# T5 attention and a feed-forward layer on one core: tail keys' scores as 64x64 products, and a bank hand-over that waits in TensorE's queue

## The chip, the cores and the metric

The kernel runs on one core of one Trainium2 chip. The metric is device time in microseconds of one execution, the median of several runs. TensorE (PE) multiplies matrices, VectorE (DVE) and ScalarE (ACT) work on rows of 128 partitions, GpSimd (POOL) and SyncE (SP) here mostly start transfers. PEld is TensorE's loading of weights, the operand that stays in the array; it overlaps with its products.

## The reference

Attention with a bias by distance for 8 batches, 8 heads, 576 positions and 64 numbers a head, then a feed-forward layer on the 4608 tokens:

```python
scores = scale * np.matmul(q, k.transpose(0, 1, 3, 2))
scores = scores + bias.transpose(2, 0, 1)[None, :, :, :]     # bias_table[bucket of |i - j|]
attn = np.exp(scores - np.max(scores, axis=-1, keepdims=True))
attn = attn / (np.sum(attn, axis=-1, keepdims=True) + 1e-09)
x = np.matmul(attn, v)            # heads side by side: 4608 x 512
h = x @ w_in                      # 512 x 2048
out = np.maximum(0.01 * h, h) @ w_out
```

## The kernel before

**Work items.** Two heads of one batch form a pair; 32 pairs n = 0 to 31 are worked through in order. Keys and queries of a pair lie transposed in SBUF, head e on partitions 64e to 64e + 63 (`kt`, `qt`). The 576 positions make four blocks of 128 (NJ = 4) and a tail of 64 (SL).

**Scores.** `score(n, u)` is `qk_mm` (TensorE) and then `exp` (ScalarE). For u = 0 to 3 it takes key block u against the first 512 queries, one product of 64 rows for each head, side by side in the array (64\*128 in the profile: rows by columns of the array). u = 4 takes all four blocks against the last 64 queries (eight small products, L314), u = 5 the 64 tail keys against all queries. For u = 5 the two heads' tail keys are put into one block-diagonal 128x128 operand by `apart` (VectorE, L284), which `transpose_k` calls; then two full-array products run, 512 and 64 columns wide (L324, L325). Scores 0, 1, 2, 3 and 5 rotate through two buffers `ps_s` of two PSUM banks each, so scores 5 wait for the exponential of scores 2.

**Values.** `av_tails` (L370) and `av_phase` (L416) multiply the exponentials with the values into one PSUM bank for each head; `divide` normalises.

**Feed-forward.** Its pieces (`ffn_in`, L468; `ffn_out`, L509) are laid between the steps of the pairs. Which kind and how many is fixed by a small planner (`plan`, `groups_of`, `two_kinds`).

**Halved pairs.** In 19 of the pairs (8, 9, 12 to 14, 17 to 19, 21 to 31) `two_kinds` chooses `body_in_halves`. There the value products, and two feed-forward pieces (`side_by_side`, L628), are split by rows of the array: the upper 64 rows work for one bank while the lower 64 work for the other, and in a second half they change over. Before the change-over the last product of the first half must have ended, because the other rows then write the same bank. `fence` puts a nop on SyncE that waits for that product, and `behind` makes the first product of the second half wait for the nop. In program order TensorE's stream of such a pair is: scores 0, value tails, first half of the values, scores 1, first products of the two feed-forward pieces, second half of the values, rest of the pieces' first half, scores 2, scores 3, the pieces' second half (four products a piece, as in the first), scores 4, one quarter of `ffn_out`, scores 5, more feed-forward work. All engines' orders are written out by hand (a manual schedule).

Functions that the change touches:

Of the kernel before, what the change touches and what calls it, by code (L numbers as in the profile page):

```python
# [37 lines left out]
def kernel(  # L38
# [10 lines left out]
    nc = tc.nc  # L49

    B, H, S, D = q.shape
# [4 lines left out]
    P = 128  # L56
    n_pairs = H // 2
    NJ = S // P
    SL = S - NJ * P
# [5 lines left out]
    n_cc = DM // P  # L65
# [178 lines left out]
    qts, kts, ops_ = {}, {}, {}  # L244
    N = len(items)
    AHEAD = 3

    prs, turned = {}, {}

# [8 lines left out]
    def by_dma(n):  # L258
        return n > 2 * n_pairs
# [22 lines left out]
    def apart(t):  # L282

        nc.vector.tensor_tensor(  # L284
            out=t[:, S : S + P].rearrange("p (e i) -> p e i", e=2),
            in0=t[:, NJ * P : S].unsqueeze(1).to_broadcast([P, 2, SL]),
            in1=own, op=ALU.mult)
# [6 lines left out]
    def transpose_k(n):  # L294
        kt = kts[n] = kts_[n % 2]
        t = turned_pair(n, 1)
        cuts = [0, -(-P // NC), RQ] if n == 0 else [0, RQ]
        for lo, hi in zip(cuts, cuts[1:]):
            nc.vector.tensor_copy(out=kt[:, lo * NC : hi * NC].rearrange("p (r c) -> p r c", c=NC),
                                  in_=t[:, lo:hi, :])  # L300
        apart(kt)

    def qk_mm(n, u, swapped=False):

        qt, kt = qts[n], kts[n]
        if u == NJ:
            if swapped:
                ps = [ps_m_pool.tile([P, 512], FP32, name="ps_q", tag="m") for e in range(2)]
            else:
                ps = [ps_o_pool.tile([P, 512], FP32, name="ps_q", tag=f"o{e}") for e in range(2)]  # L310
            for c in range(NJ):
                for e in range(2):
                    r = slice(e * D, (e + 1) * D)
                    nc.tensor.matmul(ps[e][:, c * SL : (c + 1) * SL], lhsT=kt[r, c * P : (c + 1) * P],  # L314
                                     rhs=qt[r, 512:S], start=True, stop=True)
            return ps
        ps = ps_s_pool.tile([P, 2, 512], FP32, name="ps_s")
        if u < NJ:
            for e in range(2):
                r = slice(e * D, (e + 1) * D)  # L320
                nc.tensor.matmul(ps[:, e, :], lhsT=kt[r, u * P : (u + 1) * P], rhs=qt[r, 0:512],  # L321
                                 start=True, stop=True)
        else:
            nc.tensor.matmul(ps[:, 0, :], lhsT=kt[:, S : S + P], rhs=qt[:, 0:512], start=True, stop=True)  # L324
            nc.tensor.matmul(ps[:, 1, 0:SL], lhsT=kt[:, S : S + P], rhs=qt[:, 512:S], start=True, stop=True)  # L325
        return ps

    def at_view(n):
        return at_[n % 2][:, 0:ATW].rearrange("p (e c i) -> p e c i", e=2, c=NJ)

    def exp(n, u, ps):
        at, at4 = at_view(n), at4_[n % 2]
        if u < NJ:
            nc.scalar.activation(at[:, :, u, 0:512], ps, AF.Exp, scale=scale)  # L334
        elif u == NJ:
            for e in range(2):
                nc.scalar.activation(at[:, e, :, 512:S],  # L337
                                     ps[e][:, 0 : NJ * SL].rearrange("p (c i) -> p c i", i=SL),
                                     AF.Exp, scale=scale)
        else:  # L340
            nc.scalar.activation(at4[:, 0:S], ps.rearrange("p e i -> p (e i)")[:, 0:S], AF.Exp, scale=scale)  # L341
# [54 lines left out]
    ended = mybir.DependencyInfo(mybir.DependencyClass.Sync, mybir.DependencyReason.DATA)  # L396

    def fence(sooner):

        f = nc.sync.nop(nofuse=True)  # L400
        tc.add_manual_dep(f.ins, sooner.ins.name, ended, reason="behind the last products of these rows")
        return f

    def behind(later, f):
        tc.add_manual_dep(later.ins, f.ins.name, ended, reason="the other half of the rows writes this bank")

    def av_phase(n, phase, last=None):

        b, p = items[n]
        at = at_[n % 2]  # L410
        for ic in range(NJ + 1):
            for c in range(NJ):
                for r in range(2):
                    e = r ^ phase
                    o = (e * NJ + c) * S + ic * P
                    m = nc.tensor.matmul(outs[n][e][:, ic * (D + 1) : (ic + 1) * (D + 1)],  # L416
                                     lhsT=at[halves[r], o : o + P], rhs=vn[b % NBUF][halves[r], c, 2 * p + e, :],
                                     start=False, stop=(phase == 1 and ic == NJ and c == NJ - 1))
                    if last is not None:
                        behind(m, last)  # L420
                        last = None
        return m

    def x_by_dma(n):
        return n_pairs + 2 <= n < N - 1 and n != 2 * n_pairs - 1
# [195 lines left out]
    def side_by_side(one, two):  # L621

        def phase(k, lo, hi, last=None):
            for c in range(lo, hi):
                for r in range(2):
                    pm, steps, low = one if r == k else two
                    w, x = steps[c]
                    m = nc.tensor.matmul(pm, lhsT=w[halves[r]], rhs=x[halves[r]], start=(k == 0 and c == 0),  # L628
                                         stop=(low is not None and k == 1 and c == n_cc - 1))
                    if last is not None:  # L630
                        behind(m, last)
                        last = None
            return m

        return phase
# [11 lines left out]
    def body_in_halves(n, kinds):  # L647

        late_loads = items[n][1] == 1
        if not late_loads:  # L650
            loads(n)
        turns = rows_ahead(n) if by_dma(n + 1) else []
        score(n, 0)
        av_tails(n - 1)
        last = fence(av_phase(n - 1, 0))
        score(n, 1)
        T, s = made["out"], at_piece["out"]
        if kinds[0] == "out":
            one, two = open_piece("out", (T, s)), open_piece("out", (T, s + 4))
        else:  # L660
            one, two = open_piece("in"), open_piece("out")
        phase = side_by_side(one, two)
        phase(0, 0, 1)
        av_phase(n - 1, 1, last)
        late_q = n == 2 * n_pairs
        if n + 1 < N and not late_q:
            transpose_q(n + 1)
        band(n, 0)
        divide(n - 1, range(2))
        if late_q:  # L670
            transpose_q(n + 1)
        if late_loads:
            loads(n, 1)
        last = fence(phase(0, 1, n_cc))
        score(n, 2)
        score(n, 3)
        phase(1, 0, n_cc, last)
        band(n, 1)
        if n + 1 < N:
            transpose_k(n + 1)  # L680
        score(n, 4)
        if kinds[0] == "in":
            one[2]()
        late = [n - 1]
        if x_by_dma(n - 1):
            x_transposes(late.pop())
        for m in turns:
            turn_by_dma(m)
        while stores:
            o, y = stores.pop(0)  # L690
            nc.sync.dma_start(out=o, in_=y)
        band(n, 2)
        if kinds[0] == "out":
            outs_pm[T] = one[0]
            ffn_out(T, s + 1)
            band(n, 4)
            score(n, 5)
            band(n, 5)
            ffn_out(T, s + 2)
            ffn_out(T, s + 3)  # L700
            for m in late:
                x_transposes(m, "o0")
                finished(m)
            outs_pm[T] = two[0]
            for part in range(5, 8):
                ffn_out(T, s + part)
            at_piece["out"] = (s + 8) % n_fc
            made["out"] += at_piece["out"] == 0
            return
        piece_out()  # L710
        band(n, 4)
        score(n, 5)
        band(n, 5)
        piece_out()
        piece_out()
        for m in late:
            x_transposes(m, "o1")
            finished(m)
        room["left"] -= 5
        moe(room["left"], 0)  # L720
# [91 lines left out]
    def rows_ahead(n):  # L812
        ms = [m for m in range(n + 2, min(n + AHEAD + 1, N))
              if by_dma(m) and m - (AHEAD if m > 2 * n_pairs + 2 else 2) == n]
        for m in ms:
            pair_rows(m)
        return ms
# [5 lines left out]
    def score(n, u):  # L823
        exp(n, u, qk_mm(n, u))
# [78 lines left out]
    n = n_pairs  # L903
# [25 lines left out]
    for n in range(n_pairs + 1, N + 1):  # L929
# [43 lines left out]
        while stores:  # L973
            o, y = stores.pop(0)
# [8 lines left out]
        if room["only"]:  # L983
# [6 lines left out]
            T, f = step("in")  # L990
# [54 lines left out]
```

## Time and profile before

| | |
|---|---|
| median of 3 runs | 370.56 us (370.3, 370.56, 372.05) |
| span of the profiled execution | 368.2 us |
| the profiled execution's own time | not given beside its span |
| busy: TensorE, ScalarE, VectorE, GpSimd | 97%, 67%, 53%, 20% of the span |
| granted TensorE clock | 1.000 |

The span runs from the first to the last instruction. Times are microseconds, times of single instructions nanoseconds where so marked. A row of a timeline gives start, duration, engine, line, operation, operands and a count when several instructions are merged; brackets give idle time before it and what ended it. "issue" as a releaser means that the engine waited for nothing that the profile shows. A product's duration includes its latency, so products that follow each other overlap in the record.

### The profile page before, as it was taken

The page shows a single profiled execution, that of the slowest core. Times are in us where ns is not written, and L with a number is a line of the kernel's source. Part 1 is how long each engine was busy: PE and PEld are TensorE (multiplying, and loading weights), DVE is VectorE, ACT ScalarE, POOL GpSimd, SP SyncE. Part 2 cuts the span into 40 slices and gives each one's busy share as a digit, 9 for nine tenths or more (in the row PEclk, how much of TensorE's full clock was granted, in tenths as well). Part 3 has the DMA queues.
Part 4 walks back from the last instruction along what each step waited for, and adds up shares of the span by engine and source line. Part 5 has one row for each costly group of instructions (what it writes and reads, how often), then busy time and mean ns, then how long its engine had stood idle before and what let it go on. Part 6 is the DMA issues. An engine that isn't in the chain of part 4 may idle for free.

```text
span 368.2 us, 10503 instructions
## 1 busy us (share of the span) xinstructions
PE 356.2 (97%) x4454; PEld 188.1 (51%) x4495; DVE 193.9 (53%) x503; ACT 245.3 (67%) x381; POOL 75.2 (20%) x118
## 2 busy tenths in 40 slices
PE   7989999999999999999999999999999999999996
PEld 2565565555555555555555555545555544444443
DVE  3798777667767676766765556665554200200000
ACT  5998887479847797777877777777777365055111
POOL 8755231063006300630053006100000000000000
PEclk9999999999999999999999999999999999999999
DMA  8999999979938991999199538933111000110212
GB/s 101 205 193 185 206 202 134 166 126 141 136 83 134 166 164 48 121 154 194 20 146 177 110 80 101 170 99 80 29 39 50 28 30 0 73 43 0 77 68 85
DMA packets 104358, 40.17 MB, mean 109 GB/s; under 512 B 83184, under 2 KB 98808, under 8 KB 104312
## 3 DMA queue, kind: packets, MB, share of 16 engines
q0 software_dynamic: 53696, 18.36, 49.3%
q1 hardware_dynamic: 49320, 19.06, 29.4%
q10 hardware_dynamic: 1296, 2.10, 1.6%
q8 instruction: 35, 0.57, 0.7%
q14 instruction: 11, 0.09, 0.1%
HBM read 37.68 MB, written 9.45 MB: 128 GB/s over the span
## 4 chain that ended last, share of the span: by engine, by line
PE 92%; DVE 2%; issue 2%; DMA 2%; ACT 1%; POOL 1%; ACTq 0%; POOLq 0%
PE pm L468 30%; PE pm L509 28%; PE pm L628 9%; PE ps_s L321 8%; PE ps_o L416 6%; PE ps_o L381 4%; PE ps_s L324 2%; DMA kn<-in_k_dram 2%; PE ps_o L370 1%; PE ps_q L314 1%; PE ps_tx L442 1%; PE pm L502 1%; DVE opair L392 1%; POOL qn L112 0%; PE ps_t L273 0%
## 5 line engine op out<-in xcount | busy, mean ns | idle before, releaser
L334 ACT ACTIVATE at<-ps_s 128x1024 bf16<-128x1024 f32 x128 | 124.6, 1025 | 24.6 <-PE ps_s L321 24.4
L481 ACT ACTIVATE gt<-pm 128x512 bf16<-128x512 f32 x138 | 83.2, 603 | 69.4 <-PE pm L468 68.8
L468 PE MATMUL pm<-xT,w_in_sb 128*128 128x512 bf16 x492 | 116.3, 379 | 1.0
L509 PE MATMUL pm<-w_out_sb,gt 128*128 128x512 bf16 x452 | 105.9, 379 | 3.3 <-issue 3.0
L357 DVE TENSOR_TENSOR at<-at,hk 128x768 bf16<-128x768 bf16 (+3 forms) x160 | 70.5, 454 | 52.7 <-ACT at L334 31.3
L468 PEld LDWEIGHTS <-w_in_sb 128*128 128x128 bf16 x508 | 48.0, 98 | 55.2
L509 PEld LDWEIGHTS <-gt 128*128 128x128 bf16 x476 | 43.5, 98 | 49.6
L321 PE MATMUL ps_s<-qt,kt 64*128 64x512 bf16 x256 | 43.3, 380 | 2.0 <-ACT at L334 1.6
L628 PE MATMUL pm<-w_out_sb,gt 64*128 64x512 bf16 x168 | 42.0, 376 | 0.0
L522 DVE COPY y<-pm 128x512 f32<-128x512 f32 x28 | 19.4, 692 | 40.4 <-PE pm L509 37.7
L628 PE MATMUL pm<-xT,w_in_sb 64*128 64x512 bf16 x136 | 37.5, 376 | 0.0
L392 DVE TENSOR_TENSOR opair<-ps_o,rcp 128x320 bf16<-128x320 f32 x64 | 29.7, 488 | 1.4
L119 POOL DMA_DIRECT2D vn<-in_v_dram x32 | 27.9, 879 | 10.6 <-DMA w_out_sb<-in_moe_w_out_dram 4.2
L796 POOL COPY tick<-opair 1x1 bf16<-1x1 bf16 x18 | 3.3, 181 | 131.3 <-DVE opair L392 131.3
L416 PE MATMUL ps_o<-vn,at 64*128 64x65 bf16 x1520 | 29.5, 190 | 0.0
L416 PEld LDWEIGHTS <-at 64*128 64x128 bf16 x1520 | 27.1, 94 | 4.3 <-SPq L400 3.0
L321 PEld LDWEIGHTS <-kt 64*128 64x128 bf16 x256 | 11.4, 94 | 22.5 <-issue 13.3
L341 ACT ACTIVATE at<-ps_s 128x576 bf16<-128x576 f32 x32 | 21.8, 682 | 0.3 <-PE ps_s L325 0.2
L337 ACT ACTIVATE at<-ps_q 128x256 bf16<-128x256 f32 x64 | 21.3, 395 | 0.2
L390 DVE RECIPROCAL rcp<-ps_o 128x5 f32<-128x5 f32 x64 | 10.0, 182 | 20.0 <-PE ps_o L381 16.8
L381 PE MATMUL ps_o<-vn,at 128*128 128x65 bf16 x520 | 20.2, 194 | 0.0
L381 PEld LDWEIGHTS <-at 128*128 128x128 bf16 x520 | 17.8, 98 | 3.0 <-issue 0.5
(65 smaller groups left out, 257.6 us busy)
## 6 DMA issues: line engine op xcount, KB each, us to landing
out_dram<-y SPq DMA_DIRECT2D x28, 256.0 KB, 2.7
qn<-in_q_dram POOLq DMA_DIRECT2D x14, 288.0 KB, 7.6
kn<-in_k_dram POOLq DMA_DIRECT2D x14, 288.0 KB, 9.5
vn<-in_v_dram POOLq DMA_DIRECT2D x28, 128.0 KB, 9.9
w_in_sb<-in_moe_w_in_dram POOLq DMA_DIRECT2D x2, 1024.0 KB, 11.6
w_out_sb<-in_moe_w_out_dram POOLq DMA_DIRECT2D x2, 1024.0 KB, 17.1
out_dram<-y ACTq DMA_DIRECT2D x7, 256.0 KB, 2.1
qn<-in_q_dram POOLq DMA_DIRECT2D x4, 144.0 KB, 4.5
```

The costliest lines, as they stand in the source:

```text
L119: nc.gpsimd.dma_start(out=vn[b % NBUF][:, c, h0:h1, 0:D], in_=v[b, h0:h1, c * P : (c + 1) * P, :].rearrange("h s d -> s h d"),)
L321: nc.tensor.matmul(ps[:, e, :], lhsT=kt[r, u * P : (u + 1) * P], rhs=qt[r, 0:512], start=True, stop=True)
L334: nc.scalar.activation(at[:, :, u, 0:512], ps, AF.Exp, scale=scale)
L341: nc.scalar.activation(at4[:, 0:S], ps.rearrange("p e i -> p (e i)")[:, 0:S], AF.Exp, scale=scale)
L357: nc.vector.tensor_tensor(out=o, in0=o, in1=m, op=ALU.mult)
L381: nc.tensor.matmul(ps[:, ic, :], lhsT=at[:, o : o + P], rhs=vn[b % NBUF][:, c, 2 * p + e, :], start=False, stop=(ic == NJ and c == NJ - 1))
L392: nc.vector.tensor_tensor(out=opair[:, :, e * D : (e + 1) * D], in0=ps[:, :, 0:D], in1=rcp.to_broadcast([P, NJ + 1, D]), op=ALU.mult)
L416: m = nc.tensor.matmul(outs[n][e][:, ic * (D + 1) : (ic + 1) * (D + 1)], lhsT=at[halves[r], o : o + P], rhs=vn[b % NBUF][halves[r], c, 2 * ...
L468: nc.tensor.matmul(pm, lhsT=w_in_sb[:, c, f * P : (f + 1) * P], rhs=xT[c][:, t0 : t0 + TT], start=(c == 0), stop=(c == n_cc - 1))
L481: nc.scalar.activation(g, pm, AF.Prelu, bias=0.0, scale=1.0, alpha=0.01)
L509: nc.tensor.matmul(pm, lhsT=gt[:, f, ts * P : (ts + 1) * P], rhs=w_out_sb[:, f, :], start=(f == 0), stop=(f == n_fc - 1))
L628: m = nc.tensor.matmul(pm, lhsT=w[halves[r]], rhs=x[halves[r]], start=(k == 0 and c == 0), stop=(low is not None and k == 1 and c == n_cc ...
```

## The change

Three things change, all of them for the halved pairs.

1. For these pairs, the tail keys' scores are made from the keys as they lie, with no block-diagonal operand: each head's 64 tail keys on its own 64 rows of the array, into its own 64 columns, so four 64x64 products (two of 512 and two of 64 columns) instead of two full ones. `apart` is not called for them.
2. These products move from behind the first quarter of `ffn_out` to directly behind scores 4; their exponential stays at its place in ScalarE's order.
3. The nop of a hand-over moves from SyncE's queue to TensorE's, directly ahead of the first product of the second half. Scores 2 move ahead of the last product of the feed-forward pieces' first half.

```diff
+    FIRST = 0
+    HALVED = {8, 9, 12, 13, 14, 17, 18, 19, *range(21, 31 + 1)}
...
-        apart(kt)
+        if not in_quarters(n):
+            apart(kt)
+
+    def in_quarters(n):
+        return n < FIRST or n in HALVED
...
-            nc.tensor.matmul(ps[:, 0, :], lhsT=kt[:, S : S + P], rhs=qt[:, 0:512], start=True, stop=True)
-            nc.tensor.matmul(ps[:, 1, 0:SL], lhsT=kt[:, S : S + P], rhs=qt[:, 512:S], start=True, stop=True)
+            for o, i in ((ps[:, 0, :], slice(0, 512)), (ps[:, 1, 0:SL], slice(512, S))):
+                if not in_quarters(n):
+                    nc.tensor.matmul(o, lhsT=kt[:, S : S + P], rhs=qt[:, i], start=True, stop=True)
+                    continue
+                for e in range(2):
+                    r = slice(e * D, (e + 1) * D)
+                    nc.tensor.matmul(o[e * SL : (e + 1) * SL, :], lhsT=kt[r, NJ * P : S], rhs=qt[r, i],
+                                     start=True, stop=True)
...
     def fence(sooner):
-        f = nc.sync.nop(nofuse=True)
+        return sooner
+
+    def behind(sooner):
+        f = nc.tensor.nop(nofuse=True)
         tc.add_manual_dep(f.ins, sooner.ins.name, ended, reason="behind the last products of these rows")
-        return f
-
-    def behind(later, f):
-        tc.add_manual_dep(later.ins, f.ins.name, ended, reason="the other half of the rows writes this bank")
...
     def av_phase(n, phase, last=None):
...
+                    if last is not None:
+                        behind(last)
+                        last = None
                     m = nc.tensor.matmul(...)
-                    if last is not None:
-                        behind(m, last)
-                        last = None
...
-        last = fence(phase(0, 1, n_cc))
+        phase(0, 1, n_cc - 1)
         score(n, 2)
+        last = fence(phase(0, n_cc - 1, n_cc))
         score(n, 3)
         phase(1, 0, n_cc, last)
...
         score(n, 4)
+        ps_5 = qk_mm(n, 5)
...
-            score(n, 5)
+            exp(n, 5, ps_5)
```

The edit shown in `av_phase` is made in the same way in `phase` of `side_by_side`, and the last replacement in both branches of `body_in_halves`.

More of the change, by code (lines that the diff above doesn't have):

```diff
@@ L627, in phase @@
                     w, x = steps[c]
+                    if last is not None:
+                        behind(last)
+                        last = None
                     m = nc.tensor.matmul(pm, lhsT=w[halves[r]], rhs=x[halves[r]], start=(k == 0 and c == 0),
                                          stop=(low is not None and k == 1 and c == n_cc - 1))
-                    if last is not None:
-                        behind(m, last)
-                        last = None
             return m
@@ L711, in body_in_halves @@
         band(n, 4)
-        score(n, 5)
+        exp(n, 5, ps_5)
         band(n, 5)
```

## The prediction

> **What bounds the kernel now.** I read the page first, then the busy time by stretches, then TensorE's own waits, then the timeline of one halved pair (pair 23), and last the timelines around changes of tile shape.
>
> ```profile
> span 368.2 us, 10503 instructions
> PE 356.2 (97%) x4454; PEld 188.1 (51%) x4495; DVE 193.9 (53%) x503; ACT 245.3 (67%) x381; POOL 75.2 (20%) x118
> PEclk9999999999999999999999999999999999999999
> PE 92%; DVE 2%; issue 2%; DMA 2%; ACT 1%; POOL 1%; ACTq 0%; POOLq 0%
> 62.00:285.00 223.00, 219.20 (x3237) 117.70 (x3262) 142.53 (x361) 165.25 (x253) 41.91 (x63) 1.00 0.89 114
> PE pm L509 <- issue: 3.0, 19, 0.2
> PE ps_s L321 <- ACT at L334: 1.6, 3, 0.7
> PEld L628 <- SPq L400: 3.1, 19, 0.2
> PEld L416 <- SPq L400: 3.0, 19, 0.2
> ```
>
> TensorE (PE) is busy for 97% of the span and carries 92% of the chain that ended last, at full clock throughout. The fifth line is the stretch that holds all halved pairs: TensorE 219.2 of 223.0 us, weight loads 117.7, VectorE 142.5 and ScalarE 165.3, two thirds and three quarters. So only what lengthens or shortens TensorE's stream counts. The last four lines are waits: total, times, longest. Products wait 3.0 us "for issue" and 1.6 us for ScalarE; the two lines on SyncE's nop (L400) are waits of weight loads. Nineteen pairs run halved, so each count of 19 is once per halved pair.
>
> Whether a late weight load delays a product is seen in the timeline:
>
> ```profile
> 200.22 0.53 PE L416 MATMUL ps_o<-vn,at 64*128 64x65 bf16 x24
> 200.59 0.39 PE L321 MATMUL ps_s<-qt,kt 64*128 64x512 bf16 x2
> 200.80 0.38 PE L628 MATMUL pm<-xT,w_in_sb 64*128 64x512 bf16 x1
> 200.84 0.34 PEld L416 LDWEIGHTS <-at 64*128 64x128 bf16 x8 [0.15 <-SPq L400]
> 201.02 0.26 PE L416 MATMUL ps_o<-vn,at 64*128 64x65 bf16 x6
> ...
> 202.06 0.38 PE L628 MATMUL pm<-w_out_sb,gt 64*128 64x512 bf16 x1
> 202.27 0.59 PE L321 MATMUL ps_s<-qt,kt 64*128 64x512 bf16 x4
> 202.53 0.09 PEld L628 LDWEIGHTS <-gt 64*128 64x128 bf16 x1 [0.16 <-SPq L400]
> 202.69 1.02 ACT L334 ACTIVATE at<-ps_s 128x1024 bf16<-128x1024 f32 x1 [0.56 <-PE ps_s L321]
> 202.71 0.38 PE L628 MATMUL pm<-w_out_sb,gt 64*128 64x512 bf16 x1
> ...
> 206.62 2.75 PE L468 MATMUL pm<-xT,w_in_sb 128*128 128x512 bf16 x12
> ```
>
> The last row gives the undisturbed step: (2.75 - 0.38) / 11 = 0.216 us from one 512-wide product to the next; the 0.38 of a row includes latency. Around the first hand-over the starts are 200.59, 200.80, 201.02: steps of 0.21 and 0.22. Around the second they are 202.06, 202.27 (two pairs of scores, so the next is due at 202.27 + 2 x 0.216 = 202.70) and 202.71. Both hand-overs therefore cost the products nothing: the loads wait, but behind running scores. That leaves nothing for a cheaper wait to win.
>
> **The "issue" wait.** 0.16 us, 19 times, after the last queries' scores, looks like a hole that the tail product could fill. I read it as a lost record:
>
> ```profile
> 203.57 0.28 PE L314 MATMUL ps_q<-qt,kt 64*128 64x64 bf16 x8
> 203.78 0.55 PEld L509 LDWEIGHTS <-gt 128*128 128x128 bf16 x4
> 204.01 0.81 PE L509 MATMUL pm<-w_out_sb,gt 128*128 128x512 bf16 x3 [0.16 <-issue]
> 204.65 0.38 PE L324 MATMUL ps_s<-qt,kt 128*128 128x512 bf16 x1
> 204.87 0.19 PE L325 MATMUL ps_s<-qt,kt 128*128 128x64 bf16 x1
> 204.90 1.89 PE L509 MATMUL pm<-w_out_sb,gt 128*128 128x512 bf16 x8
> ```
>
> This piece has four products (the code), four loads from 203.78, but three products in the record. The missing one fits at 204.01 - 0.216 = 203.79, just behind its load. So the array was at work there. The last three rows price the old tail product: 0.22 us for 512 columns and 0.03 for 64, 0.25 in all, in the middle of other 128*128 products.
>
> **Part 1: tail products as 64x64.** The two heads' 64x64 products sit on different rows and columns of the array, so I expect the two 512-wide ones to run together in 0.216 us and the two 64-wide ones in 0.03: 0.25 us again, no gain and no loss. Two more products and loads are issued per pair; a load hides behind the running product, as those of the undisturbed step do. What is new is the place: between the 64*128 scores and the 128*128 products there now stands a third shape. Changes of shape have a price:
>
> ```profile
> 84.55 0.28 PE L314 MATMUL ps_q<-qt,kt 64*128 64x64 bf16 x8
> 84.76 0.60 PE L468 MATMUL pm<-xT,w_in_sb 128*128 128x512 bf16 x2
> ...
> 26.20 0.45 PE L277 MATMUL ps_t<-ident,qn 96*64 96x96 bf16 x12
> 26.58 0.39 PE L324 MATMUL ps_s<-qt,kt 128*128 128x512 bf16 x1
> 26.58 0.10 PEld L324 LDWEIGHTS <-kt 128*128 128x128 bf16 x1
> L277 PE MATMUL ps_t<-ident,qn 96*64 96x96 bf16 x72 | 2.8, 217 | 0.0
> L314 PE MATMUL ps_q<-qt,kt 64*128 64x64 bf16 x256 | 9.2, 190 | 0.0
> ```
>
> 64*128 to 128*128: the last of eight scores starts at 84.55 + 0.28 - 0.19 = 84.64, its columns pass in 0.03, the next product starts at 84.76: 0.09 lost. A change of columns alone (96*64 to 128*128): the last of twelve transposes starts at 26.20 + 0.45 - 0.21 = 26.44, its 96 columns pass in 0.04 (96 of 512 columns of a 0.216 us step), and the next product starts at 26.58: 0.10 lost. Whatever the shapes, it is 0.09 to 0.10 us. No row shows 64*128 to 64*64. The bounds are 0 (only a change of rows counts) and 0.10; a gain is excluded, since 512 columns cannot pass faster than in the rows above. I take 0.097, near the upper end, because the row with a change of columns alone is the nearest. The pair had one change at this place, now it has two: 19 x 0.097 = **+1.84 us**.
>
> The two 512-wide products also write one PSUM bank at once, on different partitions. The transposes above do that from two column tiles of the same rows, at 0.04 us a pair, so they overlap; two row tiles in one bank occur nowhere in this trace. The Trainium skill says in "TensorEngine Tiling (Array Packing)", Gotcha 1 of Restrictions and Gotchas, that different row tiles cannot access the same PSUM bank at the same time. By that rule the two heads would have to go one after the other; no run here shows it yet, and it returns as a rival.
>
> The tail product needs the bank of scores 2, which the exponential 2 frees. It ends at 202.69 + 1.02 = 203.71; the tail products would come at about 203.57 + 0.28 - 0.19 + 0.03 + 0.10 = 203.79. That is tight, but scores 2 move 0.216 us ahead (part 3), and ScalarE stood idle for 0.56 us before that exponential, so it follows: 0.25 us or more of slack, no wait.
>
> **Part 2: what leaves VectorE and SyncE.**
>
> ```profile
> L284 DVE TENSOR_TENSOR kt<-kt,own 128x128 bf16<-128x128 bf16 x32 | 7.2, 225 | 1.1
> L400 SPq EVENT_SEMAPHORE  x38: 17/17/17, 63.6 to 280.2; - x38
> L370 PEldq EVENT_SEMAPHORE  x7: 51/51/51, 35.8 to 256.2; - x7
> ```
>
> VectorE loses 19 x 0.225 = 4.3 us of building block-diagonal keys: nothing on the path, since no product in these pairs waits for VectorE. SyncE loses 38 nops of 17 ns and the waits in them, so the transposes and stores behind them can only go earlier; worth nothing either, for the same reason.
>
> **Part 3: the hand-over in TensorE's own queue.** Before, 202.06 + 0.38 = 202.44 (product ends) to 202.53 (load starts) is 0.09 us: two hops of a semaphore and the 0.017 us nop, so a hop is about 0.04. After, there is one hop, then an instruction that takes TensorE 0.051 us (last row above), then the load: 0.09 us at the least, perhaps 0.12 with the first load's own issue. The new way is no faster. And behind the waiting nop stands everything else in TensorE's queue, loads that could be fetched ahead included.
>
> *First hand-over* (values): last product ends at 200.22 + 0.53 = 200.75, load at about 200.87 instead of 200.84, product due at 201.02. Hidden behind scores 1 and a pair of feed-forward products: **0**. If that cover were gone it would cost about 0.1 us each.
>
> *Second hand-over* (feed-forward): scores 2 now stand ahead of the last product, so only scores 3 (one 0.216 step) cover the wait instead of two. If the last product starts at T, the scores follow at T + 0.216, and the next half is due at T + 0.43. The product ends at T + 0.38, the load comes at T + 0.47 to 0.50, and the product goes right behind the load, as the load and product at 26.58 do. Late by 0.04 to 0.07, plus 0.01 for a start from a standstill (after the gap that precedes the scores at 199.60 below, the next step is 0.23 instead of 0.216). I take 0.06: 19 x 0.06 = **+1.14 us**. Bounds: 0 (the nop's 0.051 us lies ahead of the release) and 0.10 (a full old round trip, 0.09, plus 0.051 and 0.01): 0 to 1.9 us. A gain is excluded: there was no delay to remove.
>
> ```profile
> 199.60 0.39 PE L321 MATMUL ps_s<-qt,kt 64*128 64x512 bf16 x2
> 199.83 0.31 PE L370 MATMUL ps_o<-v,at 64*128 64x65 bf16 x10
> ```
>
> **Sum.** 1.84 + 1.14 = 3.0 us on the profiled span: 368.2 to 371.2. The page gives no other time for that execution; the median of the runs is 370.56, 2.4 us above the span, which I take as time around the first and last instruction that the change does not touch. Forecast 370.56 + 3.0 = **373.6 us**, 0.8% slower; by the bounds 370.6 to 374.5. About 0.5% (1.85 us) is what a measurement of this kernel can tell from no change, its three runs spreading from 370.3 to 372.05.
>
> **The rivals.**
>
> *A change of columns is not drained* (chance 0.15). For it: no row has 64-row tiles on both sides. Against: the 26.20 row, where rows and columns are both partial on one side. Then only the second hand-over is left: 370.6 to 372.5, likely 371.7, no measurable change.
>
> *The hole is real* (0.05, the faster side). If the 0.16 us before 204.01 is a true stall that starts when the scores end, whatever its cause, then the 0.25 us tail product moved there fills it: 19 x 0.16 = 3.0 us saved, no drain beyond the old one, hand-over as forecast or hidden: 367.6 to 368.7. It decides where the record of the fourth product is not lost but was never there in time. Against it: four loads, three products.
>
> *The halves take turns in a bank* (0.07). By a mechanism that lets one row tile at a time into a bank, 0.25 us more per pair: 19 x 0.25 = 4.7, so 378.3. The rule named in part 1 would ask for this.
>
> *An emptied queue* (0.10). Behind the first nop come 40 loads and 40 products at 0.03 us for two of each. Ten and forty products (100 instructions) passed from 199.83 to 200.59, 0.76 us. If a third of them had stood in the queue beforehand, the supply may be as slow as 0.76 / 67 = 0.0113 us; 80 of them then take 0.91 us from 200.87, against 0.73 to 201.60 now: 0.17 late, 19 x 0.17 = 3.2 us on top: 376.8. With a fuller queue ahead it would be more. The Trainium skill, "TensorE: Matmul & The Clock Gate" (table of specs), gives a queue of 64; from that, an estimate of 0.76 / 36 = 0.021 us and far over 380 would be the limit, which no row here supports.
>
> *The nop is no wait* (0.03): a wait of an engine on its own products is dropped as already in order. Then only 1.84 us is left: 372.4.
>
> **How the numbers follow.** The forecast has 0.60. Slower by over 0.5%: forecast, turns and emptied queue, 0.77, less 0.03 of the forecast for a second hand-over that is hidden after all (1.84 us, the edge): 0.74. Within 0.5%: the undrained change, the missing wait and that edge: 0.21. Faster: 0.05. The range 371.0 to 376.8 takes in the forecast's bounds, the likely part of the undrained change and the emptied queue; the case of turns and the faster one are left out.
>
> **What would show it.** Right: starts of 64*64 products about 0.10 us after the last queries' scores have passed, and the 128*128 ones again 0.10 after them; two 512-wide tail products starting within 0.01 us; first feed-forward product of the second half 0.49 us after the last of the first, not 0.43; value products at 0.43 as now. Wrong: a step of 0.43 there, no gap before the 64*64 products, tail products 0.2 apart, or value products more than 0.03 us a pair behind the nop.

## The result and the profile after

| | before | after |
|---|---|---|
| median of 4 runs each | 371.31 us (370.3 to 372.29) | 375.01 us (374.54 to 375.5) |
| span of the profiled execution | 368.2 us | 372.8 us |

The ratio is 1.0111, 95% interval 1.0078 to 1.0143: slower by 1.1%, some 4.1 us (the two medians lie 3.7 us apart, the two spans 4.6). The forecast was 3.0 us, to 373.6; the direction and both places of the loss were right, and both were priced too low.

Two groups of `ffn_out` before (count, then busy us, mean ns, then idle time before):

```profile
L509 PE MATMUL pm<-w_out_sb,gt 128*128 128x512 bf16 x452 | 105.9, 379 | 3.3 <-issue 3.0
L509 PEld LDWEIGHTS <-gt 128*128 128x128 bf16 x476 | 43.5, 98 | 49.6
```

The page after, and the same two groups:

```profile
span 372.8 us, 10600 instructions
PE 365.4 (98%) x4533; PEld 189.5 (51%) x4533; DVE 188.6 (51%) x484; ACT 245.0 (66%) x381; POOL 78.0 (21%) x118
L521 PE MATMUL pm<-w_out_sb,gt 128*128 128x512 bf16 x476 | 107.3, 379 | 0.0
L521 PEld LDWEIGHTS <-gt 128*128 128x128 bf16 x476 | 44.8, 98 | 55.1 <-issue 4.3
```

TensorE is busier and the kernel slower. In this record every load of `ffn_out` has its product, 476 and 476, and products no longer wait "for issue". The program issues the same products in both; before, 24 records are missing, and 19 of the places read as 3.0 us of idle time. The hole was not a hole; e6 and e8 below show it by the time as well.

How much a halved pair lost is read from the distance between scores 0 of pair 8 and of pair 31; 18 halved pairs start between them. TensorE's timeline, start and duration, before:

```profile
62.38 0.39 PE L321 MATMUL ps_s<-qt,kt 64*128 64x512 bf16 x2
277.31 0.39 PE L321 MATMUL ps_s<-qt,kt 64*128 64x512 bf16 x2
```

and after:

```profile
62.62 0.39 PE L327 MATMUL ps_s<-qt,kt 64*128 64x512 bf16 x2
281.74 0.39 PE L327 MATMUL ps_s<-qt,kt 64*128 64x512 bf16 x2
```

214.93 us became 219.12: 4.19 / 18 = 0.233 us a pair, 19 x 0.233 = 4.4 us. (The five other pairs between them take their old time to within 0.005 us each, so all of it falls on the halved pairs. What precedes pair 8 differs by some tenths, once by 1 us, from one profile to the next, here by 0.24 us, and is no part of the change.)

The second hand-over and the tail products of pair 23 after the change:

```profile
204.84 0.38 PE L643 MATMUL pm<-w_out_sb,gt 64*128 64x512 bf16 x1
205.05 1.02 ACT L346 ACTIVATE at<-ps_s 128x1024 bf16<-128x1024 f32 x1 [0.34 <-PE ps_s L327]
205.06 0.38 PE L327 MATMUL ps_s<-qt,kt 64*128 64x512 bf16 x2
205.35 0.09 PEld L643 LDWEIGHTS <-gt 64*128 64x128 bf16 x1 [0.41 <-issue]
205.38 0.37 PE L643 MATMUL pm<-w_out_sb,gt 64*128 64x512 bf16 x1
...
205.59 0.37 PE L643 MATMUL pm<-w_out_sb,gt 64*128 64x512 bf16 x1
205.61 0.38 PE L643 MATMUL pm<-xT,w_in_sb 64*128 64x512 bf16 x1
...
206.24 0.29 PE L320 MATMUL ps_q<-qt,kt 64*128 64x64 bf16 x8
206.46 0.43 PE L336 MATMUL ps_s<-qt,kt 64*64 64x512 bf16 x4
206.83 0.60 PE L521 MATMUL pm<-w_out_sb,gt 128*128 128x512 bf16 x2
```

- Scores 3 start at 205.06, the second half at 205.38: a step of 0.32 instead of 0.216, 0.10 us lost. The two row halves then run 0.02 apart (205.59, 205.61), where in this pair they started together before.
- The last queries' scores start at up to 206.24 + 0.29 - 0.19 = 206.34 and pass in 0.03; the 64x64 products start at 206.46: 0.09 us for the change of shape. The last of the four starts at 206.46 + 0.43 - 0.19 = 206.70, so the two heads run together (one after the other would need 0.22 more). They pass in 0.03, and from there to 206.83 is the second change, 0.10 us, which was there before as 64\*128 to 128\*128. Exponential 2, which frees their bank, ended at 205.05 + 1.02 = 206.07, 0.39 us ahead of them.

### The profile page after: what moved, and what is told of

Its sections match the earlier page's. It is cut to its first block, busy times and chain, and to the rows that moved or that the text cites. A ratio compares the mean times of both kernels' runs of the same rounds, so it can differ in the third digit from the quotient of the medians.

```text
span 372.8 us, 10600 instructions
## 1 busy us (share of the span) xinstructions
PE 365.4 (98%) x4533; PEld 189.5 (51%) x4533; DVE 188.6 (51%) x484; ACT 245.0 (66%) x381; POOL 78.0 (21%) x118
## 4 chain that ended last, share of the span: by engine, by line
PE 94%; ACT 3%; DVE 2%; issue 0%; ACTq 0%
PE pm L480 30%; PE pm L521 28%; PE pm L643 9%; PE ps_s L327 8%; PE ps_o L431 6%; PE ps_o L393 4%; PE ps_s L336 2%; ACT at L346 2%; PE ps_w L787 1%; PE ps_o L382 1%; PE ps_q L320 1%; PE ps_tx L454 1%; PE ps_s L332 1%; PE pm L514 1%; PE ps_t L279 1%; DVE opair L404 1%
## 5 line engine op out<-in xcount | busy, mean ns | idle before, releaser
L521 PE MATMUL pm<-w_out_sb,gt 128*128 128x512 bf16 x476 | 107.3, 379 | 0.0
L521 PEld LDWEIGHTS <-gt 128*128 128x128 bf16 x476 | 44.8, 98 | 55.1 <-issue 4.3
L327 PE MATMUL ps_s<-qt,kt 64*128 64x512 bf16 x256 | 46.2, 380 | 2.1 <-ACT at L346 1.8
L643 PE MATMUL pm<-w_out_sb,gt 64*128 64x512 bf16 x168 | 45.0, 375 | 0.0
L643 PE MATMUL pm<-xT,w_in_sb 64*128 64x512 bf16 x136 | 40.4, 377 | 0.0
L119 POOL DMA_DIRECT2D vn<-in_v_dram x32 | 30.9, 973 | 11.2 <-PE ps_t L275 4.2
```

Source lines behind the costliest of these rows:

```text
L119: nc.gpsimd.dma_start(out=vn[b % NBUF][:, c, h0:h1, 0:D], in_=v[b, h0:h1, c * P : (c + 1) * P, :].rearrange("h s d -> s h d"),)
L521: nc.tensor.matmul(pm, lhsT=gt[:, f, ts * P : (ts + 1) * P], rhs=w_out_sb[:, f, :], start=(f == 0), stop=(f == n_fc - 1))
```

## The experiments

The theory to be tested: two independent losses, the change of shape ahead of the 64x64 products (with some 0.02 us between the 512- and the 64-wide ones), and the second hand-over, which one step of scores no longer covers. The rivals: the hand-over with its emptied queue carries all; or the 64x64 products wait for a bank and not for a shape. The ratios compare with the kernel before on the same chip, the distances between scores 0 of pairs 8 and 31 with the 214.93 us above.

**e1: the tail products alone.**

```diff
 # the kernel before, with the 64x64 products, in_quarters and
         score(n, 4)
+        ps_5 = qk_mm(n, 5)
...
-            score(n, 5)
+            exp(n, 5, ps_5)
```

> The kernel before with the 64x64 tail products behind scores 4 alone; hand-overs and order of scores 2 as before. Theory (shape change): a halved pair gets 0.09 us ahead of the 64x64 products and 0.02 us between the 512- and the 64-wide ones, 0.11 to 0.12 us in all, so the span grows by 19 x 0.115 = 2.2 us, to about 370.4. Rival (the hand-over carries all 0.23 us of a pair, its emptied queue included): no growth, 368.2. Rival (bank: the product waits for exponential 2): scores 2 come 0.216 us later here than in the changed kernel, so the gap ahead of the 64x64 products should grow from 0.09 to 0.2 us or more.

Ratio 1.0046 (1.0015 to 1.0077), span 371.4 us. Scores 0 of pairs 8 and 31, and between them exponential 2 and the tail products of pair 23:

```profile
63.37 0.39 PE L327 MATMUL ps_s<-qt,kt 64*128 64x512 bf16 x2
...
204.87 1.02 ACT L346 ACTIVATE at<-ps_s 128x1024 bf16<-128x1024 f32 x1 [0.56 <-PE ps_s L327]
205.75 0.28 PE L320 MATMUL ps_q<-qt,kt 64*128 64x64 bf16 x8
205.96 0.43 PE L336 MATMUL ps_s<-qt,kt 64*64 64x512 bf16 x4
...
280.44 0.39 PE L327 MATMUL ps_s<-qt,kt 64*128 64x512 bf16 x2
```

217.07 us: (217.07 - 214.93) / 18 = 0.119 us a pair, 2.3 us for 19, as the theory had it. The span lies 1 us above the figure expected because this profile reached pair 8 1.0 us later. The gap ahead of the 64x64 products is 0.09 us here too (205.75 + 0.28 - 0.19 + 0.03 = 205.87 to 205.96). Exponential 2 ends at 205.89, only 0.07 us ahead of them where it was 0.39 in the changed kernel, and the gap did not grow: the bank rival fails. So does the rival by which the hand-over carries all and the tail products are free.

**e2: the hand-over and the order of scores 2 alone.**

```diff
 # the kernel before, with
+        f = nc.tensor.nop(nofuse=True)      # behind(), ahead of the first product of the second half
...
+        phase(0, 1, n_cc - 1)
         score(n, 2)
+        last = fence(phase(0, n_cc - 1, n_cc))
         score(n, 3)
```

> The kernel before with the nop on TensorE and scores 2 moved ahead of the last product; tail products as before. Theory: the second hand-over makes the second half start 0.10 us late and its two row halves run 0.02 us apart to the end of scores 4, 0.12 us a pair, 19 x 0.12 = 2.3 us, span about 370.5; the first hand-over costs nothing. Rival (all in the hand-over): 19 x 0.233 = 4.4 us, 372.6.

Ratio 1.0061 (1.0036 to 1.0085), span 370.6 us.

```profile
62.62 0.39 PE L321 MATMUL ps_s<-qt,kt 64*128 64x512 bf16 x2
...
203.68 0.38 PE L631 MATMUL pm<-w_out_sb,gt 64*128 64x512 bf16 x1
203.89 0.38 PE L321 MATMUL ps_s<-qt,kt 64*128 64x512 bf16 x2
204.18 0.09 PEld L631 LDWEIGHTS <-gt 64*128 64x128 bf16 x1 [0.41 <-issue]
204.21 0.37 PE L631 MATMUL pm<-w_out_sb,gt 64*128 64x512 bf16 x1
...
279.64 0.39 PE L321 MATMUL ps_s<-qt,kt 64*128 64x512 bf16 x2
```

217.02 us: 2.09 / 18 = 0.116 a pair, 2.2 us. With e1's 0.119 that is 0.235, the whole of the changed kernel's 0.233: the two losses add up, and neither hides a part of the other.

**e3: the nop on TensorE alone.**

```diff
 # the kernel before, with the nop of e2 and the old order:
         last = fence(phase(0, 1, n_cc))
         score(n, 2)
         score(n, 3)
```

> The kernel before with the nop on TensorE alone; scores 2 and 3 both stand behind the last product as before. Theory: two steps of scores (0.43 us) cover the wait, so nothing changes: 368.2 within 0.3. Rival (the nop itself, or the queue that it empties, costs, wherever it stands): 0.1 us or more a pair, 370 or above.

Ratio 0.9995 (0.9979 to 1.001), span 368.2 us.

```profile
62.44 0.39 PE L321 MATMUL ps_s<-qt,kt 64*128 64x512 bf16 x2
277.38 0.39 PE L321 MATMUL ps_s<-qt,kt 64*128 64x512 bf16 x2
```

214.94 us against 214.93: nothing, at either hand-over. So the rival of the emptied queue is out: 80 loads and products behind the first nop go through in their old time.

**e4: the order of scores 2 alone, the nop on SyncE.**

```diff
 # the kernel before, with
-        last = fence(phase(0, 1, n_cc))
+        phase(0, 1, n_cc - 1)
         score(n, 2)
+        last = fence(phase(0, n_cc - 1, n_cc))
```

> The kernel before with scores 2 moved ahead of the last product alone; the nop stays on SyncE. Theory: one step of cover less (0.216 us) against a slack of about 0.17 us of the load, so the second half starts 0.05 to 0.06 us late: 19 x 0.06 = 1.1 us, span about 369.3, less than with the nop on TensorE, since the queue behind the waiting load stays filled and the product follows its load at once. Rival (the hand-over by SyncE is the slower way): 0.10 us a pair or more, 370.1 or above.

Ratio 1.0033 (1.0017 to 1.0048), span 369.6 us.

```profile
62.65 0.39 PE L321 MATMUL ps_s<-qt,kt 64*128 64x512 bf16 x2
...
203.14 0.38 PE L628 MATMUL pm<-w_out_sb,gt 64*128 64x512 bf16 x1
203.35 0.38 PE L321 MATMUL ps_s<-qt,kt 64*128 64x512 bf16 x2
203.61 0.09 PEld L628 LDWEIGHTS <-gt 64*128 64x128 bf16 x1 [0.38 <-SPq L400]
203.61 0.39 PE L628 MATMUL pm<-w_out_sb,gt 64*128 64x512 bf16 x1
203.84 0.38 PE L628 MATMUL pm<-w_out_sb,gt 64*128 64x512 bf16 x1
...
278.64 0.39 PE L321 MATMUL ps_s<-qt,kt 64*128 64x512 bf16 x2
```

215.99 us: 1.06 / 18 = 0.059 a pair, 1.1 us, half of e2. From the end of the product to the next product it takes 203.61 - 203.52 = 0.09 us by SyncE and, in e2, 204.21 - 204.06 = 0.15 by TensorE's own queue: 0.12 to the load and 0.03 more to the product, where e4's product follows its load at once.

**e5: the 64x64 products at the old place.**

```diff
 # the kernel before, with the 64x64 products and in_quarters; no ps_5: in body_in_halves still
             ffn_out(T, s + 1)
             band(n, 4)
             score(n, 5)
```

> The kernel before with the 64x64 tail products at the old place, between 128*128 products of ffn_out; all else as before. Theory (shape change): one change into 64*64 and one back, where there was none, 0.093 + 0.095 us, and 0.02 us between the 512- and 64-wide products: 0.21 us a pair, 19 x 0.21 = 4.0 us, span about 372.2, more than behind scores 4. Rival (bank: the gap ahead of the 64x64 products is a wait for exponential 2): that exponential has long ended here, so no gap and 0 to 0.5 us.

Ratio 1.0109 (1.0094 to 1.0124), span 372.3 us.

```profile
62.25 0.39 PE L327 MATMUL ps_s<-qt,kt 64*128 64x512 bf16 x2
281.23 0.39 PE L327 MATMUL ps_s<-qt,kt 64*128 64x512 bf16 x2
```

218.98 us: 4.05 / 18 = 0.225 a pair against 0.21 expected, 4.3 us. Two changes of shape where none was cost 0.1 us more than the one added behind scores 4. There exponential 2 has long ended (at 205.84, with the 64x64 products at 206.87, in pair 23). Of the two places the changed kernel has the better one, and the old full product is better than either.

**e6: the full tail product moved behind scores 4.**

```diff
 # the kernel before, with
         score(n, 4)
+        ps_5 = qk_mm(n, 5)
...
-            score(n, 5)
+            exp(n, 5, ps_5)
```

> The kernel before with the full 128*128 tail products moved behind scores 4; block-diagonal keys, hand-overs and order of scores 2 as before. Theory (shape change): the change from 64*128 to 128*128 falls between scores 4 and the tail product instead of behind it, one as before: 368.2 within 0.3. Rival (bank, or the place): the tail product waits for exponential 2 as in the 64x64 case, 0.09 us a pair or more, 370 or above.

Ratio 0.9997 (0.9981 to 1.0013), span 368.4 us.

```profile
62.63 0.39 PE L321 MATMUL ps_s<-qt,kt 64*128 64x512 bf16 x2
...
203.83 0.28 PE L314 MATMUL ps_q<-qt,kt 64*128 64x64 bf16 x8
204.04 0.39 PE L324 MATMUL ps_s<-qt,kt 128*128 128x512 bf16 x1
...
277.57 0.39 PE L321 MATMUL ps_s<-qt,kt 64*128 64x512 bf16 x2
```

214.94 us: the move is free, and so is the earlier claim on the bank. The one change of shape (203.83 + 0.28 - 0.19 + 0.03 = 203.95 to 204.04, 0.09) has only moved ahead of the tail product. This run also answers the rival by which the hole is real: the tail product now stands in that place, and nothing is gained.

**e7: no cover for the second hand-over.**

```diff
 # the kernel of e2, with
         phase(0, 1, n_cc - 1)
         score(n, 2)
+        score(n, 3)
         last = fence(phase(0, n_cc - 1, n_cc))
-        score(n, 3)
```

> The kernel before with the nop on TensorE and both scores 2 and 3 ahead of the last product, so that nothing stands between it and the nop. Theory: product end to the next product's start takes 0.156 us (0.05 to the nop, 0.05 in it, 0.025 to the load, 0.03 to the product), so the second half starts 0.38 + 0.156 = 0.53 us after the last product instead of 0.216, 0.32 us late, and 0.017 us of skew between the row halves: 0.33 us a pair, 19 x 0.33 = 6.3 us, span about 374.5. Rival (a hand-over has a fixed price of about 0.12 us however it is covered): 370.5.

Ratio 1.017 (1.0146 to 1.0193), span 374.8 us.

```profile
62.60 0.39 PE L321 MATMUL ps_s<-qt,kt 64*128 64x512 bf16 x2
283.64 0.39 PE L321 MATMUL ps_s<-qt,kt 64*128 64x512 bf16 x2
```

221.04 us: 6.11 / 18 = 0.339 a pair, against 0.33 expected. (Pair 9 alone lost 0.47 us, 0.14 of it between its scores 0 and its value tails, for a cause that the record does not show; the other seventeen lost 0.33 each.) With 0.43, 0.216 and 0 us of scores in between (e3, e2, e7) the hand-over costs 0, 0.116 and 0.339: beyond the first 0.1 us of slack, each step of cover that is taken away is paid in full, so the price is not fixed.

**e8: the changed kernel with the block-diagonal keys still built.**

```diff
 # the kernel after, with
-        if not in_quarters(n):
-            apart(kt)
+        apart(kt)
```

> The changed kernel with the block-diagonal keys still built by VectorE for all pairs (0.225 us each, for nobody in the halved pairs). Theory: VectorE's 19 x 0.225 = 4.3 us are off the path, so the span is that of the changed kernel, 372.8 within 0.5. Rival (part of the change's loss is hidden by what VectorE gained): 1 us or more above that.

Ratio to the kernel before 1.0129 (1.011 to 1.0149), span 373.2 us.

```profile
63.01 0.39 PE L326 MATMUL ps_s<-qt,kt 64*128 64x512 bf16 x2
282.15 0.39 PE L326 MATMUL ps_s<-qt,kt 64*128 64x512 bf16 x2
```

219.14 us against the changed kernel's 219.12: VectorE's 4.3 us are worth nothing in the halved pairs. The 0.4 us of the span arise before pair 8 (63.01 against 62.62). The waits "for issue" are back in this record, 19 of them with 3.0 us, and with them 452 products for 476 loads, in the same distance of pairs as the changed kernel's complete record: records are missing here, and not time.

No version here beats the kernel before. e3 and e6, each a part of the change that costs nothing, equal it: they repeat its 214.93 us to 0.01, which also tells how well this distance repeats.

## Why the prediction was right, and where its sums were short

- *What bounds it, and the lost record.* Right. TensorE's stream alone counted (e8), and the 476 products of the record after, e6 and e8 show that the 0.16 us had been a lost line. The rival built on it forecast a gain.
- *Change of shape,* forecast 0.097 us: measured 0.09 by the timeline, and 64\*128 to 64\*64, which no row had shown, costs what the others do. (The row at 26.20, taken for a change of columns alone, has 96 rows against 128 as well.) The term missed about 0.02 us: I took the 512- and the 64-wide products to follow each other as the full ones do. Tail in all 0.119 (e1) for 0.097: 2.3 us instead of 1.84.
- *Two heads in one bank.* They overlap (the row at 206.46). The rule of the Trainium skill in "TensorEngine Tiling (Array Packing)", Gotcha 1, did not bind here, where the two row tiles write different partitions of the bank.
- *First hand-over,* forecast 0, and *the emptied queue,* a rival: e3 shows 0.
- *Second hand-over,* forecast 0.06 us: measured 0.116 (e2), 2.2 us instead of 1.14. This is the term that was mis-sized most. The 0.06 is what the wait costs with the old nop on SyncE (e4: 0.059), the 0.01 for a start from a standstill included: the step from 203.61 to 203.84 in e4 is 0.23, where the same step behind the nop on TensorE is 0.21 (205.38 to 205.59). In TensorE's own queue the load comes 0.12 us after the product's end, the far end of what I had allowed. Two things were left out: the product comes a further 0.03 after its load, where I had put it right behind, and the two row halves stay 0.02 us apart until scores 4 have passed. So the sign given for it, 0.49 us from the last product of the first half to the first of the second, came out as 0.54 (204.84 to 205.38).
- *Sum.* 0.119 + 0.116 = 0.235 for 0.157 a pair; 4.4 us instead of 3.0.
- *Bounds and range.* Both terms came out above the upper bound of 0.10 us that each was given, and the 375.0 us lie above the forecast's own bounds. (Their upper end is written as 374.5; its terms add up to 370.56 + 1.9 + 1.9 = 374.4.) The range reached to 376.8 only to take in the emptied queue, which e3 shows to cost nothing. The direction and the two places were understood; that the time still lies inside the range was in part luck.

Open: why the product follows its load by 0.03 us and the halves drift apart behind a nop on TensorE. That the instructions behind the nop have yet to be taken up, while those behind a waiting load stand ready, fits e2 and e4, but it was only argued. Open, too, is how much of the slower way lies in the queue and how much in the nop as an instruction, which takes TensorE 0.051 us in the record after: in no run does the load itself wait for the product, without a nop.

## What to carry to other kernels

A wait that ends behind running work costs nothing, so compare the starts of products, not the idle time of loads, and count loads against products before believing a hole. When an order is changed, count how much work is left between the event and the one that waits for it: here 0.43 us was enough, 0.216 was not. A differently shaped product belongs among its own shape; each extra shape between two others costs one more change, here 0.09 to 0.10 us.

## What the runs showed of the hardware that was not expected

- A nop in TensorE's own queue that waits for TensorE's own product was slower than the way over SyncE and back: 0.15 us from the product's end to the next product (e2) against 0.09 (e4), although no other engine takes part.
- Two 64x64 tiles on different rows and columns wrote different partitions of one bank together: 512 and 64 columns of both heads were started within 0.24 us.
- Each change of shape that was worked out cost 0.09 to 0.10 us: 64\*128 to 128\*128 and 96\*64 to 128\*128 in the kernel before, 64\*128 to 64\*64 and 64\*64 to 128\*128 in the changed one.
